# Transposing all of the attention probabilities by DMA instead of three sevenths of them on TensorE

## The chip, the cores and the metric

The kernel runs on one core of a Trainium2 chip. The metric is the device time of one execution in microseconds; lower is better. A core has TensorE (PE in the profile, with its weight loads shown apart as PEld), VectorE (DVE), ScalarE (ACT), GpSimd (POOL) and SyncE (SP), which here issues all DMAs. Every engine runs its own list of instructions in order, and waits for semaphores where an operand comes from another engine or from a DMA.

## The reference

Attention over 8 batches, 12 heads, 448 rows and 64 columns a head, with q and k normalised, then a feed-forward part with a convolution of three taps along the sequence:

```python
def rmsnorm(x, g):
    return x / np.sqrt(np.mean(x * x, axis=-1, keepdims=True) + 1e-06) * g
scores = np.matmul(rmsnorm(q, g_q), rmsnorm(k, g_k).transpose(0, 1, 3, 2)) / np.sqrt(64)
attn = np.exp(scores - np.max(scores, axis=-1, keepdims=True))
attn = attn / (np.sum(attn, axis=-1, keepdims=True) + 1e-09)
x = np.matmul(attn, v)                    # (8, 12, 448, 64), then heads side by side: (8, 448, 768)
h = np.maximum(x @ w_in, 0.0)             # 768 -> 1024
conv = sum(conv_w[k] * hp[:, k:k + S, :] for k in range(3))   # hp: h with one zero row at both ends
out = (h / (1 + np.exp(-conv))) @ w_out   # 1024 -> 768
```

All inputs and the output are float32.

## The kernel before

**Two heads at a time.** The 96 heads make 48 pairs, numbered 0 to 47, six to a batch. A pair has 2 x 448 = 896 rows of scores, which are cut into 7 slots of 128 rows. To hold float32's accuracy with float16 matmuls, a float32 operand is written as a high part (its float16 cast) and a low part (what is left, again in float16), and a product is three matmuls: high by high, low by high, high by low.

**A pair's path.** q and k are loaded, squared, summed, normalised (`square`, `square_sum`, `rsqrt`, `apply_rms`), transposed on TensorE (`qk_transpose`, line 412) and cut into parts. `scores` (line 543) makes two slots at once. For each slot `soft_max` (line 547, VectorE) takes the negative maximum, and `soft_exp` (line 555, ScalarE) the exponentials e with their row sums. The product with v needs the probabilities with their 448 columns on partitions, as 4 blocks of 112. So each slot has to be transposed, in one of two ways.

- In the first, `p_transpose` (line 585) does four float32 transposes on TensorE into PSUM, and `p_evac` copies the result to the tile PT (ScalarE or VectorE; the helper `copy`, line 77). `pv` then multiplies in float32 (line 660).
- In the second, `p_hi` casts e to float16 into a buffer ph (line 77, mostly ScalarE), `p_lo` writes the remainder beside it (the helper `binary`, line 89, GpSimd or VectorE), and `p_turn` (line 577) issues one DMA on SP that transposes the eight 128 x 128 float16 blocks of that slot into PT. `pv` takes three float16 matmuls a block (line 669).

The function `nd(n)` says how many of pair n's slots go the second way: none for pairs 0 to 7, four of seven from pair 8 on. So a pair from 8 on has both kinds of `pv`: float32 matmuls of 192 columns and float16 matmuls of 256 columns.

**v.** A batch's largest |v| gives a power of two, vsc, known after the batch's last v has been loaded. `v_scaled` (line 633, GpSimd or VectorE) multiplies v by it in place, for all pairs; from pair 8 on `v_hi` (line 77) and `v_lo` (line 89) cut the scaled v into the float16 parts vp. `x_scale` (line 676, VectorE) multiplies the result in PSUM by the reciprocal row sums, which `sum_store` (line 613) and `sum_load` (line 619) have sent through DRAM to spread them over partitions. `x_hi` and `x_lo` cut it into parts for the feed-forward matmuls.

**Feed-forward.** `in_part` (line 742) and `out_part` (line 812) are the two matmuls of a batch, between them `in_relu`, `in_conv` (line 763 for two taps), `in_tanh`, `in_gate` (line 773), `in_hi` and `in_lo` on the other engines. They run between the attention steps of the next batch; after the last pair only the feed-forward part of the last two batches is left.

**The order of the work.** A planner at the end of the function makes it while the program is built. Each step has a due time (the `at` calls, from the table `PH`), predecessors (`needs`), and engines it may run on with a cost on each (`options`). The planner simulates five engines and one DMA queue, takes the step that can start earliest, weighted by due time, and writes out every engine's list. On the chip each engine keeps to its list whatever the true times are. All buffers are rings (`BUFS`): three for e, three for ph, two for PT, two for vp, twelve for x.

Of the kernel before, what the change touches and what calls it, by code (L numbers as in the profile page):

```python
# [20 lines left out]
    T0=18.19, N0=5, T=16.2, ti=26.477, si=4.987, so=6.734, hop=0.568, beta=0.028, wi0=-41.512,  # L21
    wi1=117.871, wo0=38.32, wo1=142.628, cw=-29.146, p_evac=1.158, p_hi=2.093, p_lo=3.44,
    p_rms=1.831, p_v=1.927, p_x=0.005, p_g=2.46, p_relu=0.434, p_cv=1.228, p_qz=1.0, p_ev=8.316,
    sp=0.107, nbulk=5, p_rs=0.005, p_sq=0.882, p_w=0.5, v0=-5.896, dg=2, n1=8, sw=0, pvs=2,
    ct=1.5, p_vs=0.938, p_ph=0.39, p_pl=0.493,
# [23 lines left out]
def tile_attention_moe(ctx: ExitStack, tc, q, k, v, g_q, g_k, w_in, conv_w, w_out, out):  # L49
# [41 lines left out]
    def move(e, dst, src):  # L91
# [13 lines left out]
        qkf=3, sq=2, st=2, qT=2, kT=2, qz=2, v=8, sst=6, e=3, PT=2, x=12, c=3,  # L105
        rB=2, vacc=2, vsc=4, cwb=3, s=3, t=2, m=3, rd=2, rsum=2, rT=2, mx=10, h=2, ph=3, vp=2,
# [409 lines left out]
    def nd(n):  # L516
        return 0 if n < PH["n1"] else 2 * PH["dg"]

    def places(n):

        if ("PT", n) not in rings.setdefault("PT", Ring(BUFS["PT"])).d:
# [3 lines left out]
            t[:PB, :w].rearrange("p (k q) -> p k q", k=NB),  # L525
# [63 lines left out]
    def p_evac(n, j):  # L589
        c = SLOTS[j] - nd(n) // 2  # L590
        copy(
            on["p_evac", n, j], places(n)[0][:, :, c * P : (c + 1) * P],
            old("t", ("p", n, j))[:PB].rearrange("p (k q) -> p k q", k=NB),
        )

# [32 lines left out]
    def pvs(n):  # L628
        return (*range(0, NB, PV_STEP), *(range(NB, NB + 3) if nd(n) else ()))

    def v_scaled(n):
        v = old("v", n).rearrange("p h t d -> p (h t d)")
        elementwise(on["v_scaled", n]).tensor_scalar(  # L633
            v, v, old("vsc", n // NP)[:PB, 1:2], None, op0=ALU.mult
        )

    def v_hi(n):
        copy(on["v_hi", n], new("vp", n, [PB, 2, 2, NB, D], F16)[:, 0], old("v", n))

    def v_lo(n):  # L640
        vp = old("vp", n)
        binary(on["v_lo", n], vp[:, 1], old("v", n), vp[:, 0], ALU.subtract)

    def heads(n, k0):

        wd = nd(n) // 2 * P
# [5 lines left out]
    def pv(n, k0):  # L652
        if k0 == 0:
# [31 lines left out]
    def plan_attention(n):  # L685
# [21 lines left out]
        at(s - 6.0, v_scaled, n)  # L707
# [207 lines left out]
    def needs(name, *a):  # L915
# [62 lines left out]
        elif name == "qk_transpose":  # L978
            yield "apply_rms", *a
            yield "prepare",  # L980
# [52 lines left out]
        elif name == "p_hi":  # L1033
# [5 lines left out]
            if nd(n):  # L1039
                m, j = back(n, a[1], BUFS["ph"], nd(n))  # L1040
                yield "p_turn", m, j
# [387 lines left out]
```

## Time and profile before

Median of three runs 978.2 us (975.87 to 981.03). The profiled execution took 978.28 us, of which the span from the first to the last instruction is 976.5 us; its mean granted TensorE clock was 0.962.

| engine | busy, us | share of the span | instructions |
|---|---|---|---|
| PE | 893.8 | 92% | 6590 |
| DVE | 777.3 | 80% | 1349 |
| ACT | 680.4 | 70% | 1564 |
| POOL | 660.1 | 68% | 723 |

How to read it: PE's matmuls are pipelined, so a group's busy time runs into the next group's, and the time that a group really takes is read from the start of one to the start of the next. Three stages can be told apart: up to about 180 us the weights are converted and pairs 0 to 7 run, without DMA transposes; from 180 to 900 us pairs 8 to 47 run between the feed-forward matmuls; after 900 us only feed-forward is left. The DMA queue moved 109.82 MB in the whole execution, and SP issued 160 transposing DMAs.

### The profile page before, as it was taken

To read this page: it belongs to the slowest core of one execution; us is meant where nothing else is said; L and a number is where in the kernel's file an instruction comes from. 1 tells how busy PE (TensorE), PEld (TensorE's weight loads), DVE (VectorE), ACT (ScalarE), POOL (GpSimd) and SP (SyncE) were. 2 spreads that over 40 slices of the span, in tenths; PEclk is the share of its full clock that TensorE was granted. 3 is DMA by queue.
4 is the path that set the end of the run, shared out by engine and by line. 5 is a ranking of instruction groups with operands and counts; after the bars stand their busy time and mean duration, and the time that the engine had idled before them with its cause. 6 is when DMAs were issued, how large, how long until landed. Compare 5 with 4: busy or idle time off the path is not lost.

```text
span 976.5 us, 18886 instructions
## 1 busy us (share of the span) xinstructions
PE 893.8 (92%) x6590; PEld 522.6 (54%) x6590; DVE 777.3 (80%) x1349; ACT 680.4 (70%) x1564; POOL 660.1 (68%) x723
## 2 busy tenths in 40 slices
PE   1777688978999799999999999999999999999988
PEld 0344344545656366655665566556665665556545
DVE  6999979899689967699789977898889966992540
ACT  3678667776666777679688776788788776785331
POOL 2489868886687758498688767587778864772120
PEclk9788669998999999999999999999999999999999
DMA  9945423343773677555765667446684565244001
GB/s 215 247 105 148 126 57 76 64 101 71 155 160 75 107 125 149 116 110 103 153 133 122 125 133 148 102 92 139 144 163 92 109 148 100 51 94 107 17 16 50
DMA packets 259759, 111.02 MB, mean 114 GB/s; under 512 B 220928, under 2 KB 256080, under 8 KB 259664
## 3 DMA queue, kind: packets, MB, share of 16 engines
q1 hardware_dynamic: 259664, 109.82, 52.1%
q8 instruction: 52, 0.85, 0.3%
q14 instruction: 43, 0.35, 0.1%
HBM read 56.65 MB, written 11.18 MB: 69 GB/s over the span
## 4 chain that ended last, share of the span: by engine, by line
PE 49%; DVE 12%; POOL 6%; issue 3%; ACT 3%; DMA 1%; SPq 0%; POOLq 0%; ACTq 0%; DVEq 0%
POOL ph L89 1%; POOL gring L89 1%; POOL sq L89 1%; DMA PT<-ph 1%; DVE st L351 1%; DVE ph L89 1%; POOL x L89 1%; POOL st L386 1%; DVE c_(1_4_3520 L763 0%; POOL st L375 0%; DVE carry L788 0%; PE m_('o'_7_0_0_12066 L812 0%; PE m_('o'_5_3_0_10563 L812 0%; PE m_('o'_3_3_0_7531 L812 0%; PE m_('o'_1_3_0_4495 L812 0%
## 5 line engine op out<-in xcount | busy, mean ns | idle before, releaser
L742 PEld LDWEIGHTS <-wi 128*128 128x128 f16 x1152 | 108.7, 98 | 99.8 <-issue 16.6
L812 PEld LDWEIGHTS <-gring 128*128 128x128 f16 (+1 forms) x1056 | 101.3, 100 | 66.4 <-issue 16.9
L89 POOL TENSOR_TENSOR sq<-qkf,st 112x512 f32<-112x512 f32 x80 | 96.0, 1214 | 2.8 <-ACT wi L254 1.0
L89 POOL TENSOR_TENSOR x<-rB,x 128x448 f16<-128x448 f32 x48 | 57.2, 1191 | 49.3 <-ACT x L77 39.5
L633 POOL TENSOR_SCALAR v<-v,vsc 112x512 f32<-112x512 f32 x42 | 72.0, 1718 | 17.8 <-DVE vsc L186 16.1
L543 PEld LDWEIGHTS <-qT 64*128 64x128 f16 x864 | 32.5, 96 | 71.1 <-issue 55.5
L351 DVE TENSOR_REDUCE st<-sq 112x16 f32<-112x1024 f32 x48 | 58.0, 1209 | 3.2 <-ACT sq L345 2.4
L669 PEld LDWEIGHTS <-vp 112*64 112x64 f16 x960 | 51.1, 110 | 9.7 <-issue 7.8
L441 POOL COPY qz<-qT 64x128 f16<-64x128 f16 x90 | 37.4, 416 | 25.8 <-DVE qT L432 23.1
L89 POOL TENSOR_TENSOR vp<-v,vp 112x512 f16<-112x512 f32 x38 | 46.3, 1219 | 8.9 <-ACT vp L77 6.6
L345 ACT ACTIVATE sq<-qkf 112x1024 f32<-112x1024 f32 x33 | 34.9, 1059 | 4.5 <-DMA qkf<-in_q_dram 4.5
L89 POOL TENSOR_TENSOR sq<-qkf 112x1024 f32<-112x1024 f32 x15 | 30.1, 2005 | 4.5 <-PE t_('qk'_7_0_1418 L412 2.3
L471 DVE TENSOR_REDUCE vacc<-v 112x1 f32<-112x512 f32 x48 | 32.2, 671 | 0.3
L77 ACT CAST vp<-v 112x512 f16<-112x512 f32 x36 | 22.2, 618 | 11.4 <-PE m_('v'_18_4614 L669 3.4
L600 DVE TENSOR_SCALAR rsum<-rsum 128x7 f32<-128x7 f32 x48 | 20.8, 432 | 8.2 <-ACT e_(29_6_7231 L555 1.5
L812 PEld LDWEIGHTS <-carry 128*64 128x64 f16 x192 | 20.2, 114 | 10.8 <-issue 4.1
L375 POOL TENSOR_SCALAR st<-st 112x32 f32<-112x32 f32 (+1 forms) x53 | 19.1, 360 | 10.0 <-DVE st L388 4.2
L386 POOL TENSOR_TENSOR st<-st 112x32 f32<-112x32 f32 (+1 forms) x25 | 10.1, 406 | 22.5 <-DVE st L381 19.4
L812 PEld LDWEIGHTS <-wi 128*128 128x128 f16 (+1 forms) x192 | 19.6, 102 | 9.3 <-ACT wi L77 0.5
L788 DVE COPY carry<-gring 128x128 f16<-128x128 f16 x32 | 19.2, 599 | 5.8 <-POOL gring L89 5.8
L543 PEld LDWEIGHTS <-qz 128*128 128x128 f16 x144 | 14.1, 100 | 16.5 <-issue 6.4
L89 DVE TENSOR_TENSOR sq<-qkf,st 112x512 f32<-112x512 f32 x16 | 22.7, 1424 | 0.0
(3733 smaller groups left out, 3134.2 us busy)
## 6 DMA issues: line engine op xcount, KB each, us to landing
qkf<-in_k_dram SPq DMA_DIRECT2D x48, 224.0 KB
qkf<-in_q_dram SPq DMA_DIRECT2D x48, 224.0 KB
v<-in_v_dram SPq DMA_DIRECT2D x48, 224.0 KB
rB<-rd SPq DMA_DIRECT2D x96, 112.0 KB
wo<-in_moe_w_in_dram SPq DMA_DIRECT2D x12, 512.0 KB
gring<-in_moe_w_out_dram SPq DMA_DIRECT2D x16, 384.0 KB
PT<-ph SPq DMA_TRANSPOSE x160
rd<-rT SPq DMA_DIRECT2D x48, 3.5 KB
```

Source lines behind the costliest of these rows:

```text
L77: (nc.scalar.copy if e == "ACT" else elementwise(e).tensor_copy)(dst, src)
L89: elementwise(e).tensor_tensor(dst, a, b, op=op)
L345: nc.scalar.activation(sq, old("qkf", n), AF.Square)
L351: nc.vector.tensor_reduce(old("st", m)[:, 0, n - m].rearrange("p i s -> p (i s)"), old("sq", n).rearrange("p i h t d -> p (i h t) d"), axi ...
L441: e.tensor_copy(z[HALF[h], :, HALF[h]], old("qT", n)[HALF[h], :, t0 : t0 + 64])
L471: nc.vector.tensor_reduce(old("vacc", b)[:PB, i : i + 1], old("v", n).rearrange("p h t d -> p (h t d)"), axis=AX.X, op=ALU.max, apply_abso ...
L543: nc.tensor.matmul(ps[u][:, :S], lhs, kt[r, w], start=(i == 0), stop=(i == 2))
L600: nc.vector.tensor_scalar(r, r, 1e-9, None, op0=ALU.add)
L633: elementwise(on["v_scaled", n]).tensor_scalar(v, v, old("vsc", n // NP)[:PB, 1:2], None, op0=ALU.mult)
L669: nc.tensor.matmul(ps[HALF[h], out[h]], v[:, w, h, k], pt[:PB, a, k, col[h]], start=(i == 0 and k == 0), stop=(i == 2 and k == NB - 1),)
L742: nc.tensor.matmul(ps[:, :S], wi[:, wl, c, fc * P : (fc + 1) * P], old("x", b * NP + c)[:, xl], start=(i == 0), stop=(i == 3 * NP - 1),)
L812: nc.tensor.matmul(ps[p0 : p0 + m, :NO2], g, wo[:, wl, fc, half * NO2 : (half + 1) * NO2], start=(i == 0), stop=(i == 3 * NFC - 1),)
```

## The change

From pair 8 on all seven slots are transposed by DMA, none on TensorE. `pv` of these pairs is 24 float16 matmuls of 448 columns (line 679 of the new program) in place of 16 float32 matmuls of 192 and 24 float16 matmuls of 256. `v_scaled` is gone: `v_hi` multiplies by vsc in the instruction that casts, `v_lo` multiplies and subtracts in one instruction, which exists on VectorE alone (line 649), and for pairs 0 to 7 `x_scale` multiplies by vsc. The ring of ph has four buffers instead of three, that of x eleven instead of twelve. The planner's rules follow: a transposing DMA is costed at 1.6 instead of 2.0, a chain of DMAs on one queue no longer waits for the landing of the one before in the planner's estimate, `qk_transpose` of pair n waits for the scores of pair n - 2, and some due times and preferences of `PH` are new, so every engine's list is written in another order. Core of the diff:

```diff
-    T0=18.19, N0=5, T=16.2, ti=26.477, si=4.987, so=6.734, ...
+    T0=18.19, N0=5, T=16, ti=25.974, si=4.835, so=7.981, ... nd=[7, 7], n1=8,
...
-        qkf=3, sq=2, st=2, qT=2, kT=2, qz=2, v=8, sst=6, e=3, PT=2, x=12, c=3,
-        rB=2, ... h=2, ph=3, vp=2,
+        qkf=3, sq=2, st=2, qT=2, kT=2, qz=2, v=8, sst=6, e=3, PT=2, x=11, c=3,
+        rB=2, ... h=2, ph=4, vp=2,
...
     def nd(n):
-        return 0 if n < PH["n1"] else 2 * PH["dg"]
+        return 0 if n < PH["n1"] else PH["nd"][n % 2]
...
     def pvs(n):
-        return (*range(0, NB, PV_STEP), *(range(NB, NB + 3) if nd(n) else ()))
-
-    def v_scaled(n):
-        v = old("v", n).rearrange("p h t d -> p (h t d)")
-        elementwise(on["v_scaled", n]).tensor_scalar(
-            v, v, old("vsc", n // NP)[:PB, 1:2], None, op0=ALU.mult
-        )
+        return (
+            *(range(0, NB, PV_STEP) if nd(n) < NS else ()), *(range(NB, NB + 3) if nd(n) else ())
+        )
+
+    def width(n):
+
+        return S if nd(n) == NS else nd(n) // 2 * P
 
     def v_hi(n):
-        copy(on["v_hi", n], new("vp", n, [PB, 2, 2, NB, D], F16)[:, 0], old("v", n))
+        copy_scaled(
+            on["v_hi", n], new("vp", n, [PB, 2, 2, NB, D], F16)[:, 0], old("v", n),
+            old("vsc", n // NP)[:PB, 1:2],
+        )
 
     def v_lo(n):
         vp = old("vp", n)
-        binary(on["v_lo", n], vp[:, 1], old("v", n), vp[:, 0], ALU.subtract)
+        nc.vector.scalar_tensor_tensor(
+            vp[:, 1], old("v", n), old("vsc", n // NP)[:PB, 1:2], vp[:, 0],
+            op0=ALU.mult, op1=ALU.subtract,
+        )
...
     def x_scale(n):
-        t = old("rB", n)
-        nc.vector.tensor_tensor(t, old("m", ("v", n))[:, :S], t, op=ALU.mult)
+        t, ps = old("rB", n), old("m", ("v", n))[:, :S]
+        if nd(n):
+            nc.vector.tensor_tensor(t, ps, t, op=ALU.mult)
+        else:
+            nc.vector.scalar_tensor_tensor(
+                t, ps, old("vsc", n // NP)[:, 1:2], t, op0=ALU.mult, op1=ALU.mult
+            )
...
         elif name == "qk_transpose":
             yield "apply_rms", *a
+            yield "scores", n - 2, NG - 1
...
-            v_lo=lambda: [pool(1.16), dve(0.62)],
+            v_lo=lambda: [dve(0.69)],
...
-            p_turn=lambda: [("SP", 2.0, ("T", 1))],
+            p_turn=lambda: [("SP", 1.6, ("T", 1))],
```

Counted over the whole order, SP's list goes from 160 transposing DMAs to 280. On PE 480 float32 transposes of probabilities are gone (704 to 224). On ACT the casts of e go from 149 to 272 and the copies of transposed probabilities from 174 to 56. On POOL the remainders of e go from 133 to 262, while 42 multiplications of v and 38 remainders of v are gone. DVE gains 40 remainders of v and loses 9 remainders of e.

Three places show the new order; the names carry the pair's number and then a running number. The first is PE at the product with v of pair 30, before (m is the PSUM tile, vp the parts of v, wo32 a weight):

```order
L812 MATMUL m_('o'_3_3_1_7606<-wo32_84,wi32_83 128x384
L812 LDWEIGHTS wo32_84
L812 MATMUL m_('o'_3_3_1_7606<-wo32_84 128x384
L660 MATMUL m_('v'_30_7640<-PT_30_7346,v_30_5689 64x192 x8
L669 LDWEIGHTS vp_30_7354
L669 MATMUL m_('v'_30_7640<-PT_30_7346,vp_30_7354 64x256
```

and now:

```order
L411 MATMUL t_('qk'_33_1_7271<-ident_74,sq_33_7022 128x112 x4
L411 MATMUL t_('qk'_33_0_7279<-ident_74,sq_33_7022 128x112 x4
L679 LDWEIGHTS vp_30_6934
L679 MATMUL m_('v'_30_7293<-PT_30_6999,vp_30_6934 64x448
L679 LDWEIGHTS vp_30_6934
L679 MATMUL m_('v'_30_7293<-PT_30_6999,vp_30_6934 64x448
```

The float32 rows are gone, and the float16 rows have all 448 columns; ahead of them stand transposes of q and k of pair 33 instead of feed-forward matmuls.

The second is SP's list around the end of pair 30, before (rd and rB are the row sums on their way through DRAM, qkf and v the loads):

```order
L577 DMA_TRANSPOSE PT_30_7346<-ph1_77 128x8x128
L336 DMA qkf_34_7507<-in_q_dram 112x8x64
L613 DMA rd_30_7574<-rT_30_7528 7x128
L826 DMA out_0_dram<-c_('o'_3_2_1_7517 128x384
L577 DMA_TRANSPOSE PT_31_7603<-ph2_78 128x8x128
L619 DMA rB_30_7636<-rd_30_7574 64x448
L826 DMA out_0_dram<-c_('o'_3_3_0_7625 128x384
L577 DMA_TRANSPOSE PT_31_7603<-ph0_76 128x8x128
```

and now:

```order
L576 DMA_TRANSPOSE PT_30_6999<-ph0_76 128x8x128
L576 DMA_TRANSPOSE PT_30_6999<-ph1_77 128x8x128
L840 DMA out_0_dram<-c_('o'_3_1_1_6912 128x384
L576 DMA_TRANSPOSE PT_30_6999<-ph2_78 128x8x128
L576 DMA_TRANSPOSE PT_30_6999<-ph3_79 128x8x128
L331 DMA qkf_34_7192<-in_k_dram 112x2x256
L576 DMA_TRANSPOSE PT_30_6999<-ph0_76 128x8x128
L335 DMA qkf_34_7192<-in_q_dram 112x8x64
L617 DMA rd_30_7228<-rT_30_7115 7x128
```

Seven transposes of a pair now stand among the same loads and stores, two of them often next to each other, and the store of the row sums stands behind the pair's last transpose.

The third is POOL's list in pair 30, before (x is the attention result's parts, vsc the scale of v, st the small steps of rsqrt):

```order
L633 TENSOR_SCALAR v_30_5689<-v_30_5689,vsc_5_7163 112x512
L633 TENSOR_SCALAR v_31_5949<-v_31_5949,vsc_5_7163 112x512
L633 TENSOR_SCALAR v_32_6140<-v_32_6140,vsc_5_7163 112x512
L89 TENSOR_TENSOR vp_30_7354<-v_30_5689,vp_30_7354 112x512
L89 TENSOR_TENSOR ph0_76<-e_(30_2_7361,ph0_76 128x4x112
L441 COPY qz1_80<-qT_31_7342 64x2x64 x2
L89 TENSOR_TENSOR ph1_77<-e_(30_3_7378,ph1_77 128x4x112
```

and now:

```order
L88 TENSOR_TENSOR ph2_78<-e_(30_0_6850,ph2_78 128x4x112
L88 TENSOR_TENSOR ph3_79<-e_(30_1_6886,ph3_79 128x4x112
L88 TENSOR_TENSOR ph0_76<-e_(30_2_6927,ph0_76 128x4x112
L88 TENSOR_TENSOR ph1_77<-e_(30_3_6944,ph1_77 128x4x112
L88 TENSOR_TENSOR ph2_78<-e_(30_4_6980,ph2_78 128x4x112
L385 TENSOR_TENSOR st_32_6778<-st_32_6778 112x32
L387 TENSOR_TENSOR st_32_6778<-st_32_6778 112x32
L88 TENSOR_TENSOR x_29_7087<-rB_29_7032,x_29_7087 128x448
```

Where POOL prepared v, it now makes the remainders of e, one after the other.

More of the change, by code (lines that the diff above doesn't have):

```diff
@@ L104, in tile_attention_moe @@
     BUFS = dict(
-        qkf=3, sq=2, st=2, qT=2, kT=2, qz=2, v=8, sst=6, e=3, PT=2, x=12, c=3,
-        rB=2, vacc=2, vsc=4, cwb=3, s=3, t=2, m=3, rd=2, rsum=2, rT=2, mx=10, h=2, ph=3, vp=2,
+        qkf=3, sq=2, st=2, qT=2, kT=2, qz=2, v=8, sst=6, e=3, PT=2, x=11, c=3,
+        rB=2, vacc=2, vsc=4, cwb=3, s=3, t=2, m=3, rd=2, rsum=2, rT=2, mx=10, h=2, ph=4, vp=2,
     )
@@ L590, in p_evac @@
         c = SLOTS[j] - nd(n) // 2
-        copy(
+        args = (
             on["p_evac", n, j], places(n)[0][:, :, c * P : (c + 1) * P],
@@ L594, in p_evac @@
         )
+        if nd(n):
+            copy_scaled(*args, old("vsc", n // NP)[:PB, 1:2])
+        else:
+            copy(*args)
     def sum_step(n, i):
@@ L1046, in needs @@
             yield "pv", n - BUFS["PT"], pvs(n - BUFS["PT"])[-1]
-            yield (("p_turn", n, a[1] - 1) if a[1] else ("p_evac", n - 1, NS - 1))
+            if a[1]:
+                yield "p_turn", n, a[1] - 1
+            else:
+                yield "p_evac", n - 1, NS - 1
+                yield "p_turn", n - 1, nd(n - 1) - 1
         elif name == "p_transpose":
@@ L1157, in needs @@
             yield "out_evac", *a
+    turns = [(n, j) for n in range(NPAIR) for j in range(nd(n))]
     def back(n, g, i, m=NS):
@@ L1249, in takes @@
             return "t"
-        if name in ("in_part", "out_part") and not a[-2] or name == "pv" and not a[-1]:
+        if name in ("in_part", "out_part") and not a[-2] or name == "pv" and a[-1] == pvs(a[0])[0]:
             return "m"
@@ L1283, in enqueue @@
             waiting[e][step] = t + (PH["p_" + PATIENCE[step[0]]] if i else 0.0), c, dma
-    sys.setrecursionlimit(20000)
-    due = {}
-    def urgency(step):
-        if step not in due:
-            due[step] = min(
-                [steps[step][0]] + [urgency(p) - PH["hop"] for p in after.get(step, ())]
-            )
-        return due[step]
+    due, count = {}, dict(left)
+    line = [step for step in steps if not left[step]]
+    for step in line:
+        for p in after.get(step, ()):
+            count[p] -= 1
+            if not count[p]:
+                line.append(p)
+    assert len(line) == len(steps), [x for x in steps if count[x]][:12]
+    for step in reversed(line):
+        due[step] = min([steps[step][0]] + [due[p] - PH["hop"] for p in after.get(step, ())])
+    urgency = due.__getitem__
     LAT = {
```

53 lines of the change are left out of this document (29 added, 24 removed).

## The prediction

> **What bounds the kernel now.** First the busy times of the whole execution and the shares of the chain of waits that ended last:
>
> ```profile
> PE 893.8 (92%) x6590; PEld 522.6 (54%) x6590; DVE 777.3 (80%) x1349; ACT 680.4 (70%) x1564; POOL 660.1 (68%) x723
> ...
> PE 49%; DVE 12%; POOL 6%; issue 3%; ACT 3%; DMA 1%; SPq 0%; POOLq 0%; ACTq 0%; DVEq 0%
> ```
>
> TensorE is the busiest and holds the largest share of the chain, VectorE comes second in both, DMA hardly counts. The share is a mean over stages, so next the stage that the change touches, 180 to 900 us, in six windows (busy times of PE, PEld, DVE, ACT, POOL; granted clock; DMA share; GB/s):
>
> ```profile
> 180.00:300.00 120.00, 111.69 (x834) 64.42 (x832) 102.49 (x181) 85.89 (x201) 86.16 (x85) 0.97 0.54 112
> 300.00:420.00 120.00, 112.57 (x891) 66.76 (x890) 94.57 (x168) 85.16 (x196) 82.42 (x98) 0.99 0.62 122
> 420.00:540.00 120.00, 117.25 (x913) 70.03 (x911) 105.56 (x171) 96.27 (x219) 98.18 (x109) 1.00 0.62 125
> 540.00:660.00 120.00, 118.64 (x966) 71.92 (x966) 99.51 (x177) 91.18 (x212) 86.97 (x98) 1.00 0.57 117
> 660.00:780.00 120.00, 117.98 (x963) 71.33 (x961) 106.29 (x178) 95.47 (x222) 95.96 (x113) 1.00 0.60 129
> 780.00:900.00 120.00, 118.14 (x918) 71.87 (x913) 84.76 (x153) 86.11 (x200) 74.02 (x85) 1.00 0.49 102
> sum 720.00, PE 696.27 PEld 416.33 DVE 593.18 ACT 540.08 POOL 523.71; mean PE 116.05 PEld 69.39 DVE 98.86 ACT 90.01 POOL 87.29
> ```
>
> PE works 696 of 720 us and idles 24. So in this stage time falls if PE's work falls, until VectorE, at 593 of 720, is met. Forty pairs in 720 us make 18.0 us a pair.
>
> **What leaves PE.** The timeline of PE around pair 21 (start, duration, group); what a group takes is the distance to the next start:
>
> ```profile
> 443.15 0.65 PE L585 MATMUL t_('p'_21_6_5284<-ident,e_(21_6_5270 128*112 128x128 f32 x4
> 443.64 0.55 PE L412 MATMUL t_('qk'_23_1_5292<-ident,sq 112*128 112x112 f32 x4
> ...
> 445.42 0.36 PE L543 MATMUL s_(22_2_5318<-kT,qT 64*128 64x448 f16 x1
> ...
> 445.62 0.35 PE L543 MATMUL s_(22_2_5318<-kT,qT 64*128 64x448 f16 x1
> ...
> 446.30 1.52 PE L660 MATMUL m_('v'_21_5334<-PT,v 112*64 112x192 f32 x16
> 447.65 1.48 PE L669 MATMUL m_('v'_21_5334<-PT,vp 112*64 112x256 f16 x24
> 449.06 0.36 PE L543 MATMUL s_(22_4_5391<-kT,qT 64*128 64x448 f16 x1
> ```
>
> Transposes of one slot: 443.64 - 443.15 = 0.49 us; three slots in 40 pairs are gone: 58.8. The float32 product: 447.65 - 446.30 = 1.35 us, 40 times gone: 54.0. The float16 product of 256 columns takes 449.06 - 447.65 = 1.41; with 448 columns it is at most 1.41 x 448 / 256 = 2.47, and by the scores, where two half-array matmuls of 448 columns take 0.20, 12 x 0.20 = 2.40. I take 2.40, so 40 x 0.99 = 39.6 are added. Net: 58.8 + 54.0 - 39.6 = 73 us less on PE, 1.83 a pair, 12.2 a window. PE is left with 623 us in the stage.
>
> **What the other engines get.** Per-operation prices, from groups and from windows of one tile or line over the stage:
>
> ```profile
> L633 POOL TENSOR_SCALAR v<-v,vsc 112x512 f32<-112x512 f32 x42 | 72.0, 1718 | 17.8 <-DVE vsc L186 16.1
> L89 POOL TENSOR_TENSOR vp<-v,vp 112x512 f16<-112x512 f32 x38 | 46.3, 1219 | 8.9 <-ACT vp L77 6.6 <-PE t_('qk'_13_0_2804 L412 0.7 <-PE t_('p'_46_5_11508 L585 0.5
> 180.00:900.00 720.00, 32.62 (x38) 83.00 (x148) 149.09 (x132) 0.99 0.57 118
> 180.00:900.00 720.00, 118.42 (x1576) 42.16 (x640) 0.00 (x0) 70.03 (x120) 0.99 0.57 118
> ```
>
> The third line is the tile ph (DVE, ACT, POOL), the fourth PT (PE, PEld, DVE, ACT). POOL: 129 more remainders of e at 149.09 / 132 = 1.13 are +146; 42 multiplications of v (72.0) and 38 remainders of v (46.3) go; with some 30 us of small rsqrt steps and squares that the new order puts elsewhere, POOL stays where it was, at 524. ACT: 123 more casts at 83.00 / 148 = 0.56 are +69, 118 fewer copies at 70.03 / 120 = 0.58 are -69, and some 25 operations that come over from VectorE are about +15: 555 of the new stage, so not a bound.
>
> VectorE is the one that matters, because `v_lo` is new there. No row shows that instruction. The nearest is the convolution's tap, the same operation with two operands in SBUF, on 448 columns (line 763); beside it the least and the most that bound it:
>
> ```profile
> 180.00:900.00 720.00, 102.57 (x110) 0.99 0.57 118
> ...
> 180.00:900.00 720.00, 26.29 (x39) 0.99 0.57 118
> ...
> L89 DVE TENSOR_TENSOR vp<-v,vp 112x512 f16<-112x512 f32 x2 | 4.8, 2413 | 0.0
> L633 DVE TENSOR_SCALAR v<-v,vsc 112x512 f32<-112x512 f32 x6 | 5.1, 856 | 0.0
> ...
> 313.52 3.91 DVE L763 SCALAR_TENSOR_TENSOR c_(1_4_3520<-hbuf,cwb,c_(1_4_3520 128x448 f32<-128x448 f32 x1
> ```
>
> The tap's mean is 102.57 / 110 = 0.93, for 512 columns 1.07, 40 times 43 us. The lower bound is the remainder of k out of PSUM (line 430, second row): 0.67, or 0.77 on 512 columns, 31 us. The upper is the remainder of v when VectorE made it: 2.41, 97 us. I take 43, the row with the same operation. Off VectorE go 6 multiplications (5.1) and 2 remainders (4.8) of v and 9 remainders of e at 32.62 / 38 = 0.86 (8); what else the order moves there, fewer copies and more rsqrt steps, I put at nothing within 5. Net +25: 618 us in the stage, 4.2 a window. So VectorE's need now almost equals PE's 623.
>
> The last row is a tap that took 3.91 us. The Trainium skill ("SBUF — State Buffer", section "Who interferes with whom") says that a VectorE instruction with two SBUF inputs and a GpSimd instruction that reads SBUF block each other for a whole instruction. That row agrees; by that rule `v_lo`, which leaves GpSimd's list for VectorE's, lies nearer the upper bound, which is the second rival.
>
> **Cover.** The chain from exponential to product gets longer for the last slots: a cast, a remainder and a DMA instead of transposes and a copy. While it runs PE has feed-forward matmuls and the next pair's scores, as before. The sums behind it wait a little longer too, with the same cover.
>
> **Sum.** Windows of the stage, with the larger of PE - 12.2 and DVE + 4.2 in each: 106.7 + 100.4 + 109.8 + 106.4 + 110.5 + 105.9 = 640. Adding the 24 us that PE idled, because neither engine is ever fed perfectly: 664 instead of 720, so 56 us less. The stages before 180 and after 900 us I leave as they are: pairs 0 to 7 keep their transposes, and the last 76 us are feed-forward. The profiled execution took 978.3 (1.8 more than its span), equal to the median of 978.2: 978.3 - 56 = **922 us**.
>
> **Rivals.**
>
> *PE alone decides (A).* If feed-forward work on VectorE slides into its slack in the next window, the stage is 623 + 24 = 647, time 905. For it: the window from 780 us has VectorE at 84.76. Against: in four of six windows VectorE would be within 5 us of PE or above it.
>
> *VectorE decides (B).* `v_lo` at its upper bound makes +79 instead of +25, 13.2 a window: 115.7 + 107.8 + 118.8 + 112.7 + 119.5 + 105.9 = 680, with 24 idle 704: time 962. For it speaks the row of 3.91; against it 0.93 as the mean of 110 taps.
>
> *The DMA queue decides (C), and the kernel gets slower.* Rows: a window without transposes, the stage, its fullest piece, the start of the kernel, the issues of the transposes, and SP's timeline and the chain of waits where transposes follow each other:
>
> ```profile
> 100.00:180.00 80.00, 67.13 (x360) 34.77 (x360) 70.63 (x120) 56.13 (x130) 64.48 (x54) 0.78 0.29 75
> 180.00:900.00 720.00, 696.27 (x5468) 416.33 (x5467) 593.18 (x1022) 540.08 (x1245) 523.71 (x583) 0.99 0.57 118
> 380.00:400.00 20.00, 20.00 (x156) 12.34 (x154) 11.97 (x25) 13.30 (x30) 13.09 (x13) 1.00 0.83 166
> 0.00:40.00 40.00, 13.44 (x58) 7.08 (x59) 31.02 (x63) 18.49 (x40) 13.64 (x35) 0.99 0.97 241
> L577 SPq DMA_TRANSPOSE PT<-ph x160: 1231/1240/2233, 178.6 to 894.1; - x160
> 435.70 3.26 SPq L577 DMA_TRANSPOSE PT<-ph  x2
> 430.08 4.85 DMA PT<-ph
> ```
>
> Without transposes the DMA engines are busy 0.29 x 80 = 23.2 us for 6.0 MB, 3.9 us a MB. The stage has 0.57 x 720 = 410 us for 85 MB, of which 160 transposes of 128 x 1024 float16 are 42 MB; the other 43 MB take 167, so a transpose takes 243 / 160 = 1.52. With 120 more the stage needs 592 us of DMA, 0.89 of my 664. If the queue sustains less than 592 / 720 = 0.82, the stage is longer than before; at 0.78 it is 759, time 1017. For it: no 20 us of the stage had more than 0.83, a transpose could take 4.85 us, and SP, which issues in order, spends 1.24 us on each, 149 us more. Against: at 0.83 PE had no idle time, so nothing there was limited by DMA; at the start 0.97 was held; two transposes in a row went through SP in 3.26.
>
> A rule speaks for it. The Trainium skill ("VectorE: DVE Perf Modes", section "The three transpose paths") gives 390 ns on TensorE and 1309 ns by DMA for one 128x128 block and advises TensorE where PSUM will do; by that, 120 x 8 blocks would be an estimated 1257 us of DMA. The trace differs: eight blocks went in at most 3.26 / 2 = 1.63 us, so I give this size no chance.
>
> *The change doesn't do what it says:* excluded, the order has 280 transposing DMAs and no transpose of probabilities on PE from pair 8 on.
>
> **How the numbers follow.** Forecast (both engines near their limit, 906 to 945): 63%. A (895 to 905): 12%. B (945 to 973): 14%. C: 11%, of which 7% slower, and 4% where the queue holds about 0.82 and the time stays. The range 898 to 958 takes the forecast, most of A and about half of B, some 80%. A measurement of this kernel tells 0.5%, 4.9 us, from no change. Faster: 63 + 12 + 14 = 89%; same 4%; slower 7%.
>
> **What would show it.** Right: PE busy about 73 us less and its idle time in the stage up by at most 20 us; VectorE about 25 us more and above 90% of the stage; ACT and POOL as before; DMA share of the stage near 0.89; a pair every 16.6 us. It would be wrong if PE waits for PT or for v's product at DMA landings (C), if the remainders of v take over 2 us on VectorE (B), or if the first 180 us differ by over 10 us because of the new order. A clock below 0.95 in the stage would be a further miss: where PE idled most, it fell.
>
> ```profile
> 320.00:340.00 20.00, 15.15 (x98) 7.32 (x98) 18.50 (x32) 16.95 (x40) 14.60 (x14) 0.91 0.54 90
> ```

## The result, and the profile after

The changed kernel takes **992.8 us** (median of 3 runs, 992.08 to 993.14) where the kernel before takes 978.2: a ratio of 1.0148, 95% interval 1.0114 to 1.0183. It is 1.5% slower; 922 was forecast. The profiled execution took 993.1 us, its span is 991.4 and its mean granted clock 0.928. The busy times and the chain's shares, from its page:

```profile
PE 844.5 (85%) x5470; PEld 429.4 (43%) x5470; DVE 835.0 (84%) x1385; ACT 691.5 (70%) x1591; POOL 656.8 (66%) x709
...
PE 25%; DVE 13%; POOL 3%; issue 2%; ACT 1%; DMA 1%; POOLq 0%; ACTq 0%; DVEq 0%
```

TensorE is busy 49 us less and VectorE 58 us more; ScalarE and GpSimd stand where they stood. The six windows of the stage (columns as before):

```profile
180.00:300.00 120.00, 105.85 (x673) 51.92 (x671) 109.54 (x184) 88.75 (x204) 90.48 (x97) 0.91 0.76 149
300.00:420.00 120.00, 103.83 (x696) 52.80 (x697) 105.98 (x165) 86.95 (x201) 84.04 (x92) 0.89 0.81 157
420.00:540.00 120.00, 107.73 (x684) 52.72 (x682) 111.03 (x172) 87.32 (x204) 85.26 (x93) 0.92 0.79 157
540.00:660.00 120.00, 107.09 (x750) 54.47 (x748) 107.46 (x182) 92.62 (x212) 88.85 (x93) 0.96 0.86 164
660.00:780.00 120.00, 100.19 (x647) 49.11 (x648) 110.90 (x169) 88.90 (x206) 87.01 (x95) 0.89 0.79 155
780.00:900.00 120.00, 110.83 (x767) 57.59 (x763) 104.91 (x175) 91.27 (x211) 87.00 (x94) 0.96 0.78 152
sum 720.00, PE 635.52 PEld 318.61 DVE 649.82 ACT 535.82 POOL 522.63; mean PE 105.92 PEld 53.10 DVE 108.30 ACT 89.30 POOL 87.11
```

TensorE idles 720 - 635.5 = 84 us here, where it idled 24, and its clock is 0.89 to 0.96 instead of 0.97 to 1.00. No engine is full over 120 us: VectorE has 90%. Windows of 20 us say more. First the changed kernel over 80 us, then the kernel before in two of these windows:

```profile
520.00:540.00 20.00, 16.08 (x83) 7.03 (x81) 19.54 (x25) 11.64 (x26) 14.67 (x17) 0.83 0.61 129
540.00:560.00 20.00, 11.86 (x84) 5.59 (x82) 19.63 (x27) 16.64 (x37) 16.02 (x16) 0.83 0.63 120
560.00:580.00 20.00, 20.00 (x184) 11.25 (x179) 19.01 (x34) 15.37 (x38) 14.98 (x19) 1.00 0.97 188
580.00:600.00 20.00, 20.00 (x138) 10.48 (x137) 13.14 (x37) 14.62 (x34) 11.55 (x15) 1.00 1.02 187
```

```profile
540.00:560.00 20.00, 19.93 (x194) 12.43 (x193) 18.54 (x30) 15.72 (x39) 15.05 (x16) 1.00 0.64 112
580.00:600.00 20.00, 20.00 (x161) 12.36 (x160) 13.78 (x27) 14.58 (x34) 16.77 (x21) 1.00 0.76 148
```

From 520 to 560 us VectorE is full and TensorE starves; from 580 on TensorE is full and VectorE has 7 us to spare, which come too late for the stretch before. The same picture returns about every 110 us, once in a batch of six pairs, around the scores of its fourth and fifth pair, where VectorE has the taps of the convolution between its softmax steps. The waits of TensorE that are longest in the stage lie there (waited for, total, times, longest):

```profile
PE t_('r'_33_7916 L609 <- DVE kT L429: 5.3, 1, 5.3
PE t_('r'_27_6457 L609 <- DVE kT L429: 5.0, 1, 5.0
PE t_('r'_39_9267 L609 <- DVE kT L429: 5.0, 1, 5.0
...
PE s_(39_5_9055 L542 <- ACT e_(39_2_9042 L554: 3.5, 1, 3.5
```

Why VectorE is full there stands in the timeline of one such stretch (start, duration, group, and in brackets the idle time before it):

```profile
526.09 1.42 POOL L88 TENSOR_TENSOR sq<-qkf,st 112x512 f32<-112x512 f32 x1
...
526.53 4.43 DVE L88 TENSOR_TENSOR ph<-e_(26_6_6114,ph 128x448 f16<-128x448 f32 x1
...
527.47 1.03 POOL L88 TENSOR_TENSOR ph<-e_(27_0_6180,ph 128x448 f16<-128x448 f32 x1
...
528.47 1.03 POOL L88 TENSOR_TENSOR gring<-c_(3_3_6040,gring 128x448 f16<-128x448 f32 x1
...
529.46 1.03 POOL L88 TENSOR_TENSOR ph<-e_(27_1_6198,ph 128x448 f16<-128x448 f32 x1
...
530.44 1.43 POOL L88 TENSOR_TENSOR sq<-qkf,st 112x512 f32<-112x512 f32 x1
...
530.89 1.46 DVE L777 SCALAR_TENSOR_TENSOR c_(3_4_6144<-hbuf,cwb,c_(3_4_6144 128x448 f32<-128x448 f32 x1
...
532.27 0.61 DVE L546 TENSOR_REDUCE sst_(27_2_6226<-s_(27_2_6187 128x1 f32<-128x448 f32 x1
...
532.92 0.63 ACT L554 ACTIVATE e_(27_2_6232<-s_(27_2_6187,sst_(27_2_6226 128x448 f32<-128x448 f32 x1 [3.99 <-DVE sst_(27_2_6226 L546]
...
533.69 0.35 PE L542 MATMUL s_(27_5_6248<-kT,qT 64*128 64x448 f16 x1 [2.48 <-ACT e_(27_2_6232 L554]
```

A remainder on VectorE, 0.61 us where it is shortest, lasts 4.43 us. All that time GpSimd runs one instruction behind the other, each with two operands in SBUF. Behind the long instruction stand a tap, which takes 1.46 us, and the row maximum of pair 27's third slot; the exponential waits 3.99 us for it, and TensorE 2.48 for the exponential's buffer of scores.

### The profile page after: what moved, and what is told of

The parts are those of the page before. It is cut to its first block, busy times and chain, and to the rows that moved or that the text cites. A ratio compares the mean times of both kernels' runs of the same rounds, so it can differ in the third digit from the quotient of the medians.

```text
span 991.4 us, 17015 instructions
## 1 busy us (share of the span) xinstructions
PE 844.5 (85%) x5470; PEld 429.4 (43%) x5470; DVE 835.0 (84%) x1385; ACT 691.5 (70%) x1591; POOL 656.8 (66%) x709
## 5 line engine op out<-in xcount | busy, mean ns | idle before, releaser
L826 PEld LDWEIGHTS <-gring 128*128 128x128 f16 (+1 forms) x1056 | 103.9, 102 | 79.9 <-issue 27.0
L88 POOL TENSOR_TENSOR x<-rB,x 128x448 f16<-128x448 f32 x48 | 53.0, 1103 | 25.4 <-ACT x L76 15.9
L649 DVE SCALAR_TENSOR_TENSOR vp<-v,vsc,vp 112x512 f16<-112x512 f32 x40 | 39.7, 992 | 1.4 <-ACT vp L80 1.4
L344 ACT ACTIVATE sq<-qkf 112x1024 f32<-112x1024 f32 x36 | 37.9, 1053 | 0.7 <-DMA qkf<-in_q_dram 0.7
L372 DVE SCALAR_TENSOR_TENSOR st<-st 112x32 f32<-112x32 f32 (+1 forms) x46 | 25.4, 553 | 9.6 <-POOL st L387 6.4
L80 ACT ACTIVATE vp<-v,vsc 112x512 f16<-112x512 f32 x34 | 24.4, 719 | 7.4 <-DVE vsc L185 2.9
L88 POOL TENSOR_TENSOR sq<-qkf 112x1024 f32<-112x1024 f32 x12 | 25.7, 2140 | 5.1 <-PE t_('qk'_7_0_1417 L411 2.6
L802 DVE COPY carry<-gring 128x128 f16<-128x128 f16 x32 | 23.9, 745 | 4.6 <-POOL gring L88 4.6
L76 ACT CAST x<-rB 128x448 f16<-128x448 f32 x29 | 16.3, 561 | 12.8 <-DVE rB L687 11.9
L374 POOL TENSOR_SCALAR st<-st 112x32 f32<-112x32 f32 (+1 forms) x29 | 13.1, 450 | 8.4 <-DVE st L372 4.7
```

The source lines that it names most:

```text
L80: nc.scalar.activation(dst, src, AF.Copy, scale=scale)
L88: elementwise(e).tensor_tensor(dst, a, b, op=op)
L344: nc.scalar.activation(sq, old("qkf", n), AF.Square)
L372: v.scalar_tensor_tensor(dst, x, c, z, op0=ALU.add, op1=ALU.mult)
L649: nc.vector.scalar_tensor_tensor(vp[:, 1], old("v", n), old("vsc", n // NP)[:PB, 1:2], vp[:, 0], op0=ALU.mult, op1=ALU.subtract,)
L826: nc.tensor.matmul(ps[p0 : p0 + m, :NO2], g, wo[:, wl, fc, half * NO2 : (half + 1) * NO2], start=(i == 0), stop=(i == 3 * NFC - 1),)
```

## The experiments

**How they are read.** Beside the time, three sums over a trace: TensorE's idle time and its time at half clock between the first product matmul of pair 8 and that of pair 47 (before: 699.4 us long, 22 us idle, 10 us at half clock; after: 724.4, 84 and 113), and VectorE's excess, what its instructions last beyond the shortest of the same line, operation and shape, over the whole execution (before 190 us, after 236). All kernels were timed in three rounds beside the kernel before. D in the expectations is the theory that VectorE sets the pace at the batch boundaries, Q that the DMA queue does, O that it is the written order.

**1. Which part of the change?** The two outer taps on 16 of 448 columns (leaves out the outer taps elsewhere):

```diff
-                c, h[:, tap : tap + S], w[:, tap, fc : fc + 1], c, op0=ALU.mult, op1=ALU.add
+                c[:, :16], h[:, tap : tap + 16], w[:, tap, fc : fc + 1], c[:, :16],
+                op0=ALU.mult, op1=ALU.add,
```

> The changed kernel in its own order; the two outer taps of the convolution work on 16 of 448 columns (the rest of the output's convolution is left out), so VectorE loses up to some 115 us of its 835, every instruction stays in its place. Theory D (VectorE at the batch boundaries sets the pace, and PE's clock falls because PE starves there): PE's half-clock stretches mostly vanish, its idle time in the stage falls from about 85 us to below 40, time 910 to 940. Theory Q (the DMA queue with 280 transposes sets it): 980 to 992. Theory O (the written order itself, on any engine): within 1% of 992.8.

957.1 us, ratio 0.979 (0.977 to 0.981). VectorE's load counts: with its busy time down by 66 us (769.3), the time falls by 36, though TensorE's matmuls and the DMAs are the same. None of the three ranges was met: D had 910 to 940 with TensorE idle below 40 us, and it still idles 64. So D is right in kind, but the taps are not all of it.

The transposes with their high parts only (the low part of the probabilities is left out; the third product takes the high part in its place):

```diff
-            places(n)[1].rearrange("p a k q -> p (a k) q")[:, :, c * P : (c + 1) * P],
-            old("ph", (n, j)).rearrange("q a k p -> q (a k p)"),
+            places(n)[1][:, 0, :, c * P : (c + 1) * P],
+            old("ph", (n, j))[:, 0].rearrange("q k p -> q (k p)"),
```

> The changed kernel in its own order; each transposing DMA moves the high parts alone (4 of 8 blocks, the low by high product takes the high part a second time, so the low part's share of the result is wrong), so the DMA time of the transposes halves. Theory D: 980 to 995, DMA share of the stage falls from about 0.8 to 0.55, VectorE as before. Theory Q: 920 to 950. Theory O: within 1% of 992.8.

988.8 us, ratio 1.012 (1.009 to 1.016); idle 84 us, as after. Half of the transposed bytes are worth 4 us: Q falls.

The remainder of v on 16 of 512 columns (v's low part is left out):

```diff
-            vp[:, 1], old("v", n), old("vsc", n // NP)[:PB, 1:2], vp[:, 0],
+            vp[:, 1, 0, 0, :16], old("v", n)[:, 0, 0, :16], old("vsc", n // NP)[:PB, 1:2],
+            vp[:, 0, 0, 0, :16],
```

> The changed kernel in its own order; the remainder of v is made on 16 columns instead of 512 (the third product takes the high part of v instead, so v's low part is left out), which takes away what the change put on VectorE, some 35 us. Theory D: about half to all of those 35 us come back, 955 to 978. Theories Q and O: 988 to 993.

987.4 us, ratio 1.010 (1.007 to 1.012): the new instruction on VectorE costs 5 us. D's 955 to 978 is missed; what the change adds to VectorE's own list is at most a third of the loss.

The scaled copy of v and its remainder as before (`v_scaled` again, `v_lo` on GpSimd or VectorE), seven slots by DMA:

```diff
-            v_lo=lambda: [dve(0.69)],
+            v_scaled=lambda: [pool(1.5), dve(0.4)],
+            v_lo=lambda: [pool(1.16), dve(0.62)],
```

> All slots by DMA as in the changed kernel, but v is scaled in place and its remainder made as in the kernel before (both mostly on GpSimd); the planner writes a new order. Theory D: VectorE back to about 795 us, GpSimd up to some 770, time 950 to 980 unless GpSimd binds. Theory Q: 985 to 1000. Theory O: no forecast, the order is another.

990.8 us, ratio 1.013 (1.011 to 1.015). Undoing the half of the change that concerns v gives back 2 us and misses D's range again: GpSimd rises to 721 us, and VectorE, for which D had 795, rises with it to 857, excess 268. That was the first hint at GpSimd.

**2. The slots, the table.** Four slots of seven by DMA, all else as after:

```diff
-    nd=[7, 7]
+    nd=[4, 4]
```

> The changed kernel with its table, rules and v path, but only four of the seven slots of each pair from the ninth on are transposed by DMA, as in the kernel before; TensorE transposes the other three and the product has its float32 part again. What is left of the change is the scale of v in the cast, the remainder of v on VectorE, and the new order's table and rule. If the loss comes from the seventh to fifth slots (theory D: GpSimd gets 129 more remainders of e in close rows and holds VectorE's operations with two SBUF inputs, so that the chain of a new batch arrives late and TensorE starves and loses its clock), this is near the kernel before, 970 to 985. If the loss comes from the table, the rule or the v path (theory O), it stays at 988 or more, with TensorE's work 73 us up again.

983.3 us, ratio 1.006 (1.003 to 1.008); idle 36, half clock 17, excess 176. Most of the loss goes with the three slots; some 5 us belong to the table, the rule and v's new path.

The planner's table of the kernel before with seven slots:

> The changed kernel with the planner's table of the kernel before (costs and due times), and seven slots by DMA; the order is planned anew. Theory D: VectorE and GpSimd have the same work and meet in the same way, so the time stays within 2% of the changed kernel's 992.8 (975 to 1010) and the starved stretches at the batch boundaries remain. Theory O (the written order is what is bad): a difference of more than 2% either way, and starved stretches in other places or none.

1015.8 us, ratio 1.039 (1.035 to 1.044), idle 88 and half clock 102. The difference of 2.3% is beyond the 2% that was set for O, so the order counts, but it does not cure. The new table is 23 us better for seven slots than the old one, and both starve.

Four slots for even pairs, seven for odd ones (`nd=[4, 7]`):

> The changed kernel, but only every second pair from the ninth on has all seven slots transposed by DMA; the others have four. Theory D, with the loss in proportion to the added remainders: half way between the kernel with four everywhere and the changed one. A saving for TensorE that is not yet eaten by VectorE would put it below both, 950 to 970. Theory O: 985 to 995, as the changed kernel.

982.6 us, ratio 1.003 (1.001 to 1.005). Not half way (988), and not below both: as four everywhere, so the loss is not in proportion to the added remainders.

**3. GpSimd's rows.** The remainder of e on 16 of 448 columns; the low part of the probabilities is left out, all DMAs and matmuls stay:

```diff
-            on["p_lo", n, j], ph[:, 1, :, :PB],
-            old("e", (n, j)).rearrange("q (k p) -> q k p", k=NB), ph[:, 0, :, :PB], ALU.subtract,
+            on["p_lo", n, j], ph[:, 1, 0, :16],
+            old("e", (n, j))[:, :16], ph[:, 0, 0, :16], ALU.subtract,
```

> The changed kernel in the same order, but the remainder of e is computed on 16 of its 448 columns only (the rest of the low part stays zero), so that GpSimd's and VectorE's remainders cost a tenth or so; left out is the low part of the probabilities. DMA, TensorE and ScalarE keep all their work. Theory D: with GpSimd's long rows gone, VectorE's operations are held less; its time above the least for each operation falls from 238 us to below 190, TensorE's idle time in the stage falls from 85 to below 50 us, its clock comes back, and the time is 925 to 960. Theory O: VectorE has about 30 us less of its own work and no more than that changes; the time is 970 or more and the stretches at the batch boundaries stay starved.

926.9 us, ratio 0.948 (0.944 to 0.951): idle 39, half clock 44, excess 117. VectorE lost 126 us of busy time, though only 18 of the 280 remainders were its own.

That cut does two things: it takes rows off GpSimd, and it shortens the chain from exponential to transpose. Three runs part them. In the first two a dummy stands behind each cut remainder that GpSimd makes, in the same order, on constants, with nobody waiting for it: a subtraction that reads SBUF, or two memsets that only write (the buffers `mx`, which hold one number for each weight or batch, go from 10 to 5 for space).

```diff
+        if on["p_lo", n, j] == "POOL":
+            nc.gpsimd.tensor_tensor(
+                ddst.rearrange("p (k q) -> p k q", k=4),
+                ident[:, :112].unsqueeze(1).to_broadcast([P, 4, 112]),
+                ident.bitcast(F16)[:, :112].unsqueeze(1).to_broadcast([P, 4, 112]),
+                op=ALU.subtract,
+            )
```

> The kernel with the remainder of e cut to 16 columns (926.9), and behind each cut remainder on GpSimd a subtraction of full size (128x448) that reads constants in SBUF and writes a buffer that nobody reads: GpSimd's list is as long as in the changed kernel, but the chain from exponential to transpose does not contain it. As before the low part of the probabilities is left out. D1, the long rows hold VectorE's operations with two SBUF inputs: 975 or more, VectorE's time above the least of each operation back over 200 us, TensorE idle and half clock at the batch boundaries again. D2, the longer chain (a remainder of 1.1 us between cast and transpose, and the buffers of e held by it) is what counted: 945 or less.

```diff
+        if on["p_lo", n, j] == "POOL":
+            nc.gpsimd.memset(ddst, 0.0)
+            nc.gpsimd.memset(ddst, 0.0)
```

> As the kernel before it, but the dummy work on GpSimd is two memsets of 128x448 float16 (about 0.5 us each by the rows of the program's start), which write SBUF and read nothing. If VectorE is held only by GpSimd's reading (D1 with the rule that reading blocks), this is at 940 or less, with VectorE's excess below 150 us. If it is GpSimd's occupancy (its small steps of the square roots and gates come later) or any use of the port, it is as long as the kernel with the dummy subtraction.

998.8 us with the subtractions (ratio 1.022, 1.017 to 1.027), 939.1 with the memsets (0.961, 0.957 to 0.965). The busy rows of the page, of the cut kernel, then with the reading dummy and its group, then with the writing dummy and its groups:

```profile
PE 821.4 (89%) x5470; PEld 423.4 (46%) x5470; DVE 709.1 (77%) x1385; ACT 685.8 (74%) x1591; POOL 427.9 (46%) x709
```

```profile
PE 840.4 (84%) x5470; PEld 428.1 (43%) x5470; DVE 833.7 (84%) x1385; ACT 692.0 (69%) x1591; POOL 704.0 (71%) x971
...
L575 POOL TENSOR_TENSOR ddst<-ident x262: 1008/1020/1508, 168.8 to 916.2; 128x448 f16<-128x448 f32 x131
```

```profile
PE 825.6 (88%) x5470; PEld 425.0 (45%) x5470; DVE 723.9 (77%) x1385; ACT 687.3 (73%) x1591; POOL 656.0 (70%) x1233
...
L575 POOL MEMSET ddst<- x262: 461/471/515, 169.4 to 859.0; 128x448 f16 x131
L576 POOL MEMSET ddst<- x262: 471/471/719, 170.0 to 859.5; 128x448 f16 x131
```

VectorE executes the same 1385 instructions in all three. With 262 reading rows of 1.02 us on GpSimd they take 124.6 us longer, 0.48 us a row; with 0.94 us of memsets in each place they take 14.8 us longer. The kernel gets 72 us longer with the first and 12 with the second, though GpSimd is busy nearly as long (704 and 656 us). So D2 is rejected, and it is mainly the reading of SBUF that counts, not GpSimd's occupancy and not the chain of the probabilities. One line shows the mechanism on one kind of instruction, the two outer taps (VectorE busy, count, from 180 to 840 us; cut, with reading, with writing):

```profile
180.00:840.00 660.00, 82.81 (x106) 0.97 0.88 172
```

```profile
180.00:840.00 660.00, 107.50 (x92) 0.94 0.80 158
```

```profile
180.00:840.00 660.00, 86.07 (x106) 0.96 0.86 168
```

A tap lasts 0.78, 1.17 and 0.81 us. The row maxima, whose input lies in PSUM and not in SBUF, are the counter-test (same columns, same order):

```profile
180.00:840.00 660.00, 167.02 (x274) 0.97 0.88 172
```

```profile
180.00:840.00 660.00, 151.00 (x249) 0.94 0.80 158
```

```profile
180.00:840.00 660.00, 162.40 (x267) 0.96 0.86 168
```

They last 0.61 us in all three.

The third run puts the dummy subtraction into the kernel before, behind its 120 evacuations of transposed probabilities from pair 8 on, and changes nothing else but `mx`, from 10 to 5 as well (not run alone; the cut kernel with the memsets has it too, at 939.1 us):

> The kernel before in its own order, with a dummy subtraction of 128x448 on GpSimd behind each of the 120 evacuations of transposed probabilities from pair 8 on: GpSimd gets the 120 rows that the change gives it, and nothing else is changed. D1: slower, 990 to 1010, with VectorE's busy time up by 20 to 45 us and TensorE losing clock where it starves. D2 or O: within 0.5% of the kernel before, since nobody waits for these rows.

1044.6 us, ratio 1.070 (1.063 to 1.076), more than expected. 120 rows that nobody waits for cost 65 us, 0.54 us each, and VectorE's busy time rises by 64:

```profile
PE 908.6 (87%) x6590; PEld 523.6 (50%) x6590; DVE 841.2 (81%) x1349; ACT 681.8 (66%) x1564; POOL 776.3 (75%) x843
```

What part of the 65 runs through GpSimd's own later steps, behind the added rows, is not separated in this kernel.

**4. The control.** The cut of the remainders, which gave 926.9 us, in the kernel before (the low part of these probabilities is left out here too):

> The control: the kernel before with the remainder of e cut to 16 of 448 columns in the same way (160 remainders; the low part of these probabilities is left out). If the 66 us that the cut gave the changed kernel are the price of GpSimd's rows only where TensorE has been relieved, the kernel before, bound by TensorE, gains at most its 24 us of idle time: 955 to 975; then the change without these rows is worth 30 to 50 us, near its forecast. If it gains as much per row (160/280 of 66, 38 us: about 940), the change is worth 10 to 15 us even without them.

965.6 us, ratio 0.986 (0.984 to 0.988), idle 11. The kernel before gains 14 us where the changed one gains 66. So the change alone, with the remainders cut on both sides, is worth 965.6 - 926.9 = 39 us of the 56 forecast, and GpSimd's remainders turn these 39 into a loss of 15.

**5. Is the lost clock a cause?** Fillers ahead of the transpose of the sums in each batch's fourth pair. In the first try they wrote columns of the scores' tile:

> The changed kernel in the same order, with 45 matmuls of 64 columns into unused PSUM columns ahead of the transpose of the sums of the fourth pair of each batch, where TensorE stands still for 4 to 5 us and then works at half clock; they wait for nothing and fill that hole. If the lost clock is a cause of its own, the half-clock time behind these holes goes and the kernel gets 5 to 20 us faster (973 to 988). If it only follows from TensorE having nothing to do (VectorE sets the pace of these stretches), the time stays within 4 us of 992.8 although the clock is higher.

1000.6 us, ratio 1.022 (1.019 to 1.024), but inconclusive: the fillers themselves waited up to 5.5 us for a row maximum and left the holes open (half clock 102). The second try wrote columns of the output tile that nobody reads:

```diff
+        if n >= 9 and n % NP == 3:
+            kt = filler["kt"]
+            for _ in range(120):
+                nc.tensor.matmul(
+                    filler["m"][:, NO2 : NO2 + 64], kt[:, 0, :P], kt[:, 0, :64],
+                    start=False, stop=False,
+                )
```

> The changed kernel in the same order, with 120 matmuls of 64 columns (33 ns each by the run before, some 4 us) ahead of the transpose of the sums of each batch's fourth pair; they write columns of the running output tile that nobody reads, and so wait for nothing, where those of the run before waited for a row maximum and left the holes open. If the lost clock is a cause of its own, the half-clock time behind these holes goes and the kernel gets 5 to 20 us faster (973 to 988). If it only follows from the starvation, 989 or more although the clock is higher.

996.5 us, ratio 1.018 (1.015 to 1.021). The stage's clock rises, as this row shows (PE, PEld, DVE, ACT, POOL, clock, DMA share, GB/s), from 0.92 to 0.96, the time at half clock falls from 113 to 61 us, and the kernel is not faster:

```profile
180.00:900.00 720.00, 647.48 (x5024) 343.82 (x5022) 642.49 (x1038) 533.60 (x1229) 520.89 (x556) 0.96 0.81 155
```

So the higher clock behind these holes gives nothing that shows in the time, as the reading of starvation has it. The fillers are themselves 33 us of work for TensorE, and 61 us at half clock remain, so it is not shown that the lost clock costs nothing anywhere.

**6. A better version.** Four slots only where TensorE starves (fourth and fifth pair of each batch, `nd=[7, 7, 7, 4, 4, 7]`):

> The changed kernel, but the fourth and fifth pair of each batch (from pair 8 on), in whose stretch TensorE idles and VectorE is full, have only four slots transposed by DMA and three by TensorE; the other four pairs of a batch keep seven. If the loss is local to these stretches (D), TensorE's transposes fall into its idle time there and GpSimd's list gets shorter where it hurts: 955 to 975, below both kernels. If the share of DMA slots counts wherever it is (as half of them did: 982.6), 980 to 990.

985.2 us, ratio 1.007 (1.004 to 1.009). It gives 8 us, not 18 to 38, and lies where the reading was that the share counts wherever it is: VectorE's busy time is 811 us, and TensorE's transposes now wait there too (5.6 us at most).

Then work was taken off VectorE and GpSimd and given to ScalarE (the carry's copies, the middle of q, the rms factor where VectorE had it), and the addition of 1e-9 dropped, which changes nothing in float32 because a sum that contains exp(0) is at least 1:

```diff
-            apply_rms=lambda: [pool(1.2), dve(0.94)],
+            apply_rms=lambda: [pool(1.2), act(2.0)],
-            q_middle=lambda: [pool(0.37), dve(0.15)],
+            q_middle=lambda: [act(0.3)],
-            in_carry=lambda: [dve(0.32)],
+            in_carry=lambda: [act(0.3)],
```

> A version meant to be faster, with the full computation: the changed kernel with work taken from VectorE and GpSimd and given to ScalarE, which is busy 70%: the copies for the carry (VectorE, 32 at 0.74 us) and of the middle of q (86 on GpSimd at 0.41, 10 on VectorE at 0.60), the rms factor where VectorE had it (18 at 1.32), and without the addition of 1e-9 to sums that are at least 1 (48 at 0.44, no change in float32). VectorE loses some 70 us of its own and GpSimd 35. If VectorE sets the pace (D1), the time falls as with the cut of the taps or more: 945 to 965. If the starved stretches come from the order's latencies, 985 or more.

987.0 us, ratio 1.007 (1.005 to 1.010): outside both expectations. The trace shows where: from the product of pair 8 to that of pair 47 it is 694 us instead of 724, but the product of pair 8 starts at 217.6 us instead of 194.5. The guess was that ScalarE is the wrong place at the start. So the same, from pair 8 and the second batch on:

> As the lighter version (987.0; from pair 8 on its stage is 30 us shorter than the changed kernel's, 694 instead of 724, but the first 200 us are 23 longer), with the moves to ScalarE only from pair 8 on (the middle of q, the rms factor) and for all batches but the first (the carry). If VectorE's relief in the stage is what counts, the start comes back to about 195 us and the time is 960 to 970. If the 23 us at the start and the 30 in the stage are the same work in another place, 980 or more.

**970.0 us**, ratio 0.992 (0.989 to 0.995), the full computation, 0.8% faster than the kernel before and 23 us faster than the changed one. The product of pair 8 starts at 199.0 us, so the guess held. That VectorE's relief gives the 23 us is not shown: its busy time is 825 us, only 10 less, because the new order has it make 41 of the 280 remainders of e instead of 18; GpSimd makes 239 instead of 262. The copies for the carry show what the move of one operation does. In the changed kernel (least, median, most, in ns):

```profile
L802 DVE COPY carry<-gring x32: 177/806/2858, 170.8 to 889.4; 128x128 f16<-128x128 f16 x32
```

In this version:

```profile
L76 ACT COPY carry<-gring x24: 280/294/307, 387.3 to 868.0; 128x128 f16<-128x128 f16 x24
L76 DVE COPY carry<-gring x8: 181/904/1345, 176.5 to 223.9; 128x128 f16<-128x128 f16 x8
```

On VectorE a copy of 0.18 us takes 0.8 in the middle; on ScalarE all take 0.29.

With four and seven slots in turn:

> The same, with four slots by DMA for every second pair from the ninth on and seven for the others. GpSimd has 60 remainders less, TensorE some 37 us more. If VectorE and GpSimd are still what bounds the starved stretches, this is faster than seven everywhere: 950 to 965. If TensorE is the bound again after the relief, it is slower than seven everywhere by up to 20.

979.6 us, ratio 1.001 (0.998 to 1.003): slower than seven everywhere by 10, as was expected for the case that TensorE is the bound again. VectorE's busy time is 785 us, 39 less than with seven, and does not help.

## Why the prediction was wrong

**What leaves PE** was right in its prices. The product of 448 columns takes 540.20 - 537.81 = 2.39 us (forecast 2.40):

```profile
537.81 2.46 PE L679 MATMUL m_('v'_26_6282<-PT,vp 112*64 112x448 f16 x24
540.20 1.31 PE L756 MATMUL m_('i'_3_7_6234<-x,wi 128*128 128x448 f16 x6
```

The busy time fell by 49 and not by 73 while 113 us ran at half clock; in the kernel with the remainders cut, where it is 44 us and the matmuls are the same, it fell by 72 (to 821.4).

**What the other engines get.** ScalarE and GpSimd did not become bounds (536 and 523 in the stage, 555 and 524 forecast). The bet on `v_lo` was right too, 0.99 us for 1.07:

```profile
L649 DVE SCALAR_TENSOR_TENSOR vp<-v,vsc,vp 112x512 f16<-112x512 f32 x40 | 39.7, 992 | 1.4 <-ACT vp L80 1.4
```

But "Net +25" for VectorE was +57 in the stage (593.2 to 649.8). The step that failed is the one that priced GpSimd's 129 new remainders on GpSimd alone. They lengthen VectorE's other instructions: of the 58 us that VectorE gained over the whole execution, 46 are excess (190 to 236), some 10 of them in `v_lo` itself (0.99 us, 0.73 at best). The two outer taps, quoted at 0.93 us, now take 119.31 / 106 = 1.13.

```profile
180.00:900.00 720.00, 119.31 (x106) 0.92 0.80 156
```

The 9 remainders that left VectorE, put at 8 us, brought nothing: the tile ph (DVE, ACT, POOL) took 32.62 us of VectorE in 38 instructions and now takes as much in 26.

```profile
180.00:900.00 720.00, 32.54 (x26) 146.10 (x262) 284.42 (x252) 0.92 0.80 156
```

The prediction had the row of 3.91 us in hand and used it for `v_lo` alone. That GpSimd's total did not change was no protection; which of its rows hold VectorE, and when, was not asked.

**Cover and sum.** "The larger of PE and DVE in each window" was taken over 120 us, more than a whole batch, which mixes the stretch where VectorE is full with the one where TensorE is. The same sum over the 36 windows of 20 us of the same trace, with the same terms, is 670 us instead of 640, 694 with the idle time: 952. With VectorE at +57 it is 688 and 712: 970. So of the 71 us between 922 and 993, about 30 are the window's width and 18 VectorE's term; the last 23 no sum of busy times accounts for; that they are waits of the two engines for each other within 20 us is argued, not shown. This splits a sum and not the causes: by the control, GpSimd's remainders cost the changed kernel 66 us and the kernel before 14, a difference of 52, more than the 18 of VectorE's term. "The 24 us that PE idled" became 84.

**The rivals.** B had the right engine for the starved stretches with the wrong price: VectorE sets the pace there, though not through `v_lo`, and the time went beyond the 962 given for it. C is rejected: DMA kept 0.80 of 720 us, 576 (592 were forecast), all waits of TensorE's matmuls ahead of the products sum to 0.3 us between pairs 8 and 47 (those of its weight loads at DMA landings to 1.8), and half the bytes changed 4 us. The 1.63 us that the prediction read for eight blocks are SP's issues and not the transfers, which landed a median of 3.5 us after their issue; the DMA engines' time, on which C rests, came out near the forecast. A is rejected: TensorE idled 84 us of the stage and was the full engine only in between, as from 580 to 600 us.

**The rule that was cited.** The Trainium skill ("SBUF — State Buffer", section "Who interferes with whom") says that a VectorE instruction with two SBUF inputs contends with a GpSimd instruction that reads SBUF and not with one that only writes. The runs agree: 0.48 us of VectorE for each reading row of 1.02 us, 14.8 us in all for the writing ones. The prediction cited it and let it bear on one instruction of the several kinds that it concerns: taps, remainders, gates, the steps of the square roots.

**The signs named in advance** did their work: VectorE's +25, TensorE's idle time (60 us more, for at most 20) and the clock of 0.95 failed at first sight, waits at DMA landings and `v_lo` above 2 us did not come (786 ns in the middle, 2331 at most), and that left VectorE's other instructions.

## What to carry to other kernels

A row on GpSimd that reads SBUF is not free, even when nobody waits for it: here each cost VectorE about 0.5 us of its 1.0, against 0.6 us at best for the same remainder made on VectorE itself; price such moves on both engines. When the bound engine is relieved, look for the next bound in windows shorter than the program's period, since a mean over a batch hides a stretch in which the other engine is already full. A fallen TensorE clock in such a stretch is a sign and need not be a cause: raising it here gave nothing.

## What was unexpected of the hardware

VectorE can be held not for one GpSimd instruction but for a row of them: 4.43 us, through four that follow each other without a gap. Copies of float16 with a single input get longer too: 177 ns at best, 806 in the middle, 2858 at most. The kernel with the remainders cut has this row, and below it stand those with the reading and with the writing dummy:

```profile
L802 DVE COPY carry<-gring x32: 179/194/1868, 172.0 to 824.3; 128x128 f16<-128x128 f16 x32
```

```profile
L810 DVE COPY carry<-gring x32: 179/208/3020, 171.2 to 894.1; 128x128 f16<-128x128 f16 x32
```

```profile
L806 DVE COPY carry<-gring x32: 178/427/1869, 171.8 to 838.2; 128x128 f16<-128x128 f16 x32
```

By the median the writing dummy lengthens these copies more than the reading one, the other way round than for the taps; what lengthens them in the changed kernel is open.

And a transposing DMA did not get slower when there were 280 of them instead of 160: by the marks of completion in the traces a median of 3.5 us from issue to landing before, 3.3 after.
